# Attention's product with V: from two rounded fp32 parts per head to plain fp32 in four column tiles

## The chip, the cores and the metric

The kernel runs on one core of one Trainium2 chip. Its time is the device time of one execution in microseconds (us). Engines are named as in the profile: PE is TensorE's matmul, PEld its weight load, DVE is VectorE, ACT is ScalarE, POOL is GpSimd, SP is SyncE, whose queue issues nearly all DMAs.

## What is computed

A block of attention with a memory over four segments, and behind it a channel MLP, all in float32. The change touches only `a_dot`, the product of the softmax with V:

```python
# x: (1, 2048, 1024); H = 32 heads of Dh = 32; N = 4 segments of L = 512
h = x + _A_ref(_layernorm(x), wq, wk, wv, wo, beta)
out = h + _B_ref(_layernorm(h), w1, b1, w2, b2)

# _A_ref, for each segment s
logits = jnp.einsum("bhqd,bhkd->bhqk", qs, ks) * scale + mask     # causal
p = _softmax(logits, axis=-1)
a_dot = jnp.einsum("bhqk,bhkd->bhqd", p, vs)
pq = phi(qs)
a_mem = (pq @ M) / (pq @ z + 1e-6)
o = g * a_mem + (1.0 - g) * a_dot                                 # g = sigmoid(beta), per head
M = M + phi(ks).T @ vs;  z = z + phi(ks).sum()
# at the end: concat(o) @ wo
```

## The kernel before

**Units.** The sequence is done in two halves of two segments each. Attention of a half runs over 8 groups of four heads, and in a group over its two segments: 16 units a half, 32 in all. A unit is one group in one segment. Its dense part (`dense`, L432) projects K, Q and V, 24 steps of three 512-column matmuls each (L124 to L126, one for each pair of a rounded high part and a rest). While it runs, the heads of the unit before are done beside it: `interleave` (L816) takes one step of `heads` after each dense step. Further work of a unit hangs on these steps by the table `TIMES` (L33): at step `ck`, for instance, the key weights of the next group are cast, at `lk` they are loaded.

**A head.** Each head takes a slot of six steps, and the table `HEAD` (L34) says at which step each of its operations stands; a number of 6 or more means a later slot, in which the next head has already begun. `qk` (L652) makes the logits for four blocks of 128 queries (128 to 512 keys each), adds the mask on DVE and takes the exponential on ACT. `ptr` (L696) transposes the weights `pr` in three groups into PSUM banks `ppt`, 10 transposes a head. ACT rounds each group into `pth` (float32r), and `sub` (L714) has DVE put the rest into `ptl`. `av` (L718) multiplies: for each of four blocks of keys, `vs` stands as weights, 64 columns that hold V's rounded part (32) and its rest (32), and `pth` and `ptl` stream through, 8 matmuls a head into the bank `po`. ACT copies the lower half of `po` into `ot` (L734), and `av_out` (L736) adds the upper half on DVE. At the fourth head POOL multiplies `ot` by `w` (L743). `weigh` (L681) makes `w`, which holds gate over sum for each query: a transpose `pw`, a copy, a DMA out to `r_dram` (L691) and four DMAs back (L693).

**Small matmuls.** Reading and updating the memory M takes 24 small matmuls in a unit that has both (`pm`, `pmm`, L425). They are kept in a list, and `one_small` takes one of them in front of a transpose (10 places a head) or of a product (7 places).

**What sets the order.** Engines take their instructions in the order of the program, which a scheduler may change where dependencies leave it room; `in_order` (L104) fixes the written order. The attention units ran without it.

Of the kernel before, what the change touches and what calls it, by code (L numbers as in the profile page):

```python
# [17 lines left out]
P = 128  # L18
# [11 lines left out]
RA, RH, RS, PD, PS = 1.3, 14, 0.7, 20, 3  # L30
VT, KT, OT = True, True, True
WLC = 8
TIMES = dict(pk=10, kx=12, pkh=21, pkl=22, ks=11, qs=16, pq=16, pqh=20, pql=20, omt=20, vx=24, pm=25, vs=32, vl=33, pmm=40, om=35, omc=40, od=62, lk=13, lq=16, lv=20, ck=18, cq=22, cv=28)  # L33
# [14 lines left out]
def build(tc, x, wq, wk, wv, wo, beta, w1, b1, w2, b2, out):  # L48
# [52 lines left out]
        getattr(nc, lo_eng).tensor_tensor(lo, w, raw(hi), op=ALU.subtract)  # L101

    @contextmanager
    def in_order(*engines):  # L104
# [12 lines left out]
        acts["last"] = last  # L117

    def behind(op):

# [232 lines left out]
    def attention(half, first):  # L353
# [293 lines left out]
                yield  # L647

        offs = [0, 128, 384, 768]
        koff = [0, 512, 1024, 896]  # L650

        def qk(st, i):  # L652
            u, j = st["u"], st["j"]
# [41 lines left out]

        def ptr(st, n):  # L696
            grp = ((0,), (1, 3), (2,))[n]
            if n == 0:
                st["pth"] = ab.tile([P, 1280], F32R, name="pth", bufs=2)
                st["ptl"] = ab.tile([P, 1280], F32R, name="ptl", bufs=2)  # L700
            pr, pth, ptl = st["pr"], st["pth"], st["ptl"]
            ppt = psum.tile([P, 512], F32, tag="pt", name="ppt", bufs=2)
            base = koff[grp[0]]
            w = 0
            for jk in grp:
                for i in range(jk, 4):
                    one_small()
                    o = koff[jk] - base + (i - jk) * P
                    nc.tensor.transpose(ppt[:, o:o + P], pr[:, offs[i] + jk * P:offs[i] + (jk + 1) * P], ident)  # L709
                    w += P  # L710
            acts["pth"] = n, nc.scalar.copy(pth[:, base:base + w], ppt[:, :w])  # L711
            st["sub", n] = (ptl[:, base:base + w], ppt[:, :w], raw(pth[:, base:base + w]))

        def sub(st, n):  # L714
            o, x0, x1 = st["sub", n]
            nc.vector.tensor_tensor(o, x0, x1, op=ALU.subtract)  # L716

        def av(st, n):  # L718
            u, j = st["u"], st["j"]
            if n == 0:  # L720
                st["po"] = psum.tile([P, 512], F32, tag="av", name="po", bufs=1)[0:64, :]
            po = st["po"]
            for jk in (0, 1) if n == 0 else (3, 2):
                w = 512 - P * jk
                v = u["vs"][:, 4 * j + jk, :]
                for part in ("pth", "ptl"):
                    if (jk, part) != (3, "ptl"):
                        one_small()
                    nc.tensor.matmul(po[:, P * jk:], v, st[part][:, koff[jk]:koff[jk] + w],  # L729
                                     start=(jk, part) == (0, "pth"), stop=(jk, part) == (2, "ptl"))  # L730
            if n == 1:
                if j == 0:
                    u["ot"] = ab.tile([P, 512], F32, name="ot", bufs=1)
                nc.scalar.copy(u["ot"][32 * j:32 * j + 32, :], po[32:64, :])  # L734

        def av_out(st):  # L736
            u, j, po = st["u"], st["j"], st["po"]
            ot = u["ot"]
            b = slice(32 * j, 32 * j + 32)
            nc.vector.tensor_tensor(ot[b, :], po[0:32, :], ot[b, :], op=ALU.add)  # L740
# [18 lines left out]

        stages = int(max(HEAD.values())) // 6  # L760
        pipe = [None] * stages
        fns = {"q": qk, "r": inverse, "w": weigh, "t": ptr, "s": sub, "a": av, "o": av_out}

        def slot(cur):
            states = [cur] + pipe
# [836 lines left out]
```

## Time and profile before

| What | Value |
|---|---|
| Median of the three runs shown | 2276.23 us |
| Lowest and highest run | 2275.69 and 2284.74 us |
| Profiled execution: span, first to last instruction | 2272.7 us |
| Attention of the first half, first and last product with V | 58.7 and about 539 us |
| Attention of the second half, first and last product with V | about 919 and 1396.7 us |
| DVE rows of L716 (`ptl`) | 384 of 595 ns mean |
| ACT rows of L711 (`pth`) | 384 of 512 ns mean |

The page gives the span of the profiled execution; what lies around it is seen only as the distance to the median, 3.5 us. A line of the page's groups reads: source line, engine, operation, output and inputs by the program's names, forms, count; then busy time and mean duration of one in ns; then how long the engine sat idle ahead of them, and what ended that. In a timeline the columns are start and duration in us, engine, line, operation and form; like neighbours stand in one row with their count.

### The profile page before, as it was taken

What the parts mean: (1) busy time and instruction counts of PE and PEld (TensorE: products, weight loads), DVE (VectorE), ACT (ScalarE), POOL (GpSimd) and SP (SyncE); (2) the same over time, 40 slices, a digit from 0 to 9 for tenths busy, and PEclk for the clock granted to TensorE, in tenths of its full rate; (3) what the DMA queues carried; (4) which work ended last, traced back from release to release, by engine and by line L of the source; (5) the groups of instructions that cost most, each with busy time, mean ns of one, the idle gap of its engine ahead of it and who ended that gap; (6) DMA issues with size and microseconds to landing.
All of it is one profiled execution on the core that took longest, in us unless ns stands there. A gap on an engine that the chain in (4) does not pass through costs nothing.

```text
span 2272.7 us, 34849 instructions
## 1 busy us (share of the span) xinstructions
PE 2243.7 (99%) x11481; PEld 1861.9 (82%) x11481; DVE 1541.0 (68%) x3073; ACT 1232.8 (54%) x2553; POOL 856.8 (38%) x710
## 2 busy tenths in 40 slices
PE   8999999999999999999999999999999999999999
PEld 6888888877888888888888887888888888888887
DVE  6777777776656565777777787655666766567653
ACT  6777777774453445777777775453334223222221
POOL 4232233334244442233333334244445654055430
PEclk9999999999999999999999999999999999999999
DMA  6666666665475655666655565466568975476762
GB/s 215 182 190 181 181 179 176 177 177 196 139 212 165 189 167 173 195 177 179 178 173 169 178 195 189 142 210 181 162 177 310 331 253 197 155 257 226 244 234 89
DMA packets 400798, 437.41 MB, mean 192 GB/s; under 512 B 33102, under 2 KB 267114, under 8 KB 400618
## 3 DMA queue, kind: packets, MB, share of 16 engines
q1 hardware_dynamic: 337450, 398.48, 56.8%
q10 hardware_dynamic: 63168, 36.71, 5.4%
q8 instruction: 91, 1.49, 0.3%
q14 instruction: 89, 0.73, 0.1%
HBM read 287.41 MB, written 128.78 MB: 183 GB/s over the span
## 4 chain that ended last, share of the span: by engine, by line
PE 86%; DMA 4%; POOL 3%; ACT 2%; DVE 2%; issue 1%; SPq 1%; POOLq 0%; ACTq 0%; DVEq 0%
PE po L1436 22%; PE bps L1040 10%; PE cps L1040 7%; PE dps L1040 7%; PE po L729 6%; PE ppt L709 5%; PE pqk L659 3%; PE qps L124 3%; PE qps L125 2%; PE kps L124 2%; PE qps L126 2%; PE vps L124 2%; PE kps L126 2%; PE kps L125 2%; PE vps L125 2%; PE vps L126 2%
## 5 line engine op out<-in xcount | busy, mean ns | idle before, releaser
L668 ACT ACTIVATE pr<-pr,mx 128x128 f32<-128x128 f32 (+3 forms) x512 | 289.1, 565 | 107.3 <-DVE mx L660 104.0
L660 DVE CUSTOM_DVE_ANT_0 pr<-pqk,mask 128x128 f32<-128x128 f32 (+3 forms) x512 | 247.2, 484 | 87.0 <-PE pqk L659 82.2
L711 ACT CAST pth<-ppt 128x512 fp32r<-128x512 f32 (+1 forms) x384 | 194.9, 512 | 91.3 <-PE ppt L709 88.9
L716 DVE TENSOR_TENSOR ptl<-ppt,pth 128x512 fp32r<-128x512 f32 (+1 forms) x384 | 226.8, 595 | 14.5 <-ACT pth L711 11.9
L709 PE MATMUL ppt<-ident,pr 128*128 128x128 f32 x1280 | 217.4, 276 | 0.7 <-DVE ptl L716 0.4
L1446 DVE TENSOR_TENSOR c<-c,po 128x512 f32<-128x512 f32 x160 | 105.4, 683 | 149.0 <-PE po L1436 147.2
L709 PEld LDWEIGHTS ppt<-ident,pr 128*128 128x128 f32 x1280 | 163.9, 140 | 36.7 <-issue 2.2
L659 PE MATMUL pqk<-ks,qs 96*128 96x128 f32 (+3 forms) x512 | 183.0, 358 | 1.1 <-DVE mx L660 1.1
L799 POOL TENSOR_TENSOR wl<-wr,wh 128x1024 fp32r<-128x1024 f32 x42 | 101.1, 2406 | 179.1 <-ACT wh L797 132.0
L729 PE MATMUL po<-ptl,vs 128*64 128x512 f32 (+3 forms) x512 | 153.1, 308 | 1.9 <-DVE ptl L716 1.9
L729 PE MATMUL po<-pth,vs 128*64 128x512 f32 (+3 forms) x512 | 147.8, 309 | 2.9 <-DVE ot L740 1.6
L1436 PE MATMUL po<-w2h,zh 128*128 128x512 f32 x378 | 121.0, 390 | 0.2 <-DVE zh L1376 0.2
L1040 PE MATMUL bps<-zh,sb 128*128 128x512 f32 x336 | 111.1, 391 | 0.0
L1293 POOL TENSOR_TENSOR w2r<-w2r 128x512 f32<-128x512 f32 x54 | 85.4, 1590 | 68.3 <-DMA w2r<-in_B_w 45.4
L1040 PE MATMUL bps<-zh,sa 128*128 128x512 f32 x336 | 110.9, 391 | 0.0
L124 PE MATMUL kps<-yh,wh 128*128 128x512 f32 (+1 forms) x264 | 109.9, 416 | 0.0
L124 PE MATMUL qps<-yh,wh 128*128 128x512 f32 x256 | 107.8, 421 | 0.0
L124 PE MATMUL vps<-yh,wh 128*128 128x512 f32 x256 | 106.2, 415 | 0.0
L659 PEld LDWEIGHTS pqk<-ks,qs 96*128 96x128 f32 x512 | 98.2, 192 | 8.3 <-DVE mx L660 1.8
L1436 PE MATMUL po<-w2h,hl 128*128 128x512 f32 x322 | 103.3, 390 | 0.4 <-DVE hl L1376 0.4
L125 PE MATMUL kps<-yl,wh 128*128 128x512 f32 (+1 forms) x264 | 102.8, 389 | 0.1
L126 PE MATMUL kps<-yh,wl 128*128 128x512 f32 (+1 forms) x264 | 102.9, 390 | 0.0
(251 smaller groups left out, 6527.8 us busy)
## 6 DMA issues: line engine op xcount, KB each, us to landing
hr<-h_dram SPq DMA_DIRECT2D x112, 448.0 KB, 5.3
w2r<-in_B_w SPq DMA_DIRECT2D x122, 256.0 KB, 4.3
r<-in_B_w SPq DMA_DIRECT2D x56, 512.0 KB, 4.5
ks<-ks_dram SPq DMA_DIRECT2D x128, 192.0 KB, 3.1
h_dram<-ht ACTq DMA_DIRECT2D x84, 256.0 KB, 3.7
ks_dram<-kh SPq DMA_DIRECT2D x64, 256.0 KB, 2.6
wr<-in_A_wo SPq DMA_DIRECT2D x32, 512.0 KB, 4.5
wx<-in_B_w SPq DMA_DIRECT2D x56, 256.0 KB, 3.5
```

The costliest lines, as they stand in the source:

```text
L124: nc.tensor.matmul(ps, ah, bh, start=first, stop=False)
L125: nc.tensor.matmul(ps, ah, bl, start=False, stop=False)
L126: acts["mm"] = nc.tensor.matmul(ps, al, bh, start=False, stop=last)
L659: nc.tensor.matmul(pqk[:, :n], u["qs"][j][:, i * P:(i + 1) * P], u["ks"][j][:, 0:n], start=True, stop=True)
L660: nc.vector.tensor_tensor_reduce(out=st["pr"][:, offs[i]:offs[i] + n], in0=pqk[:, :n], in1=mask[:, 512 - n:512], op0=ALU.add, op1=ALU.min, ...
L668: nc.scalar.activation(pi, pi, AF.Exp, bias=mx[:, i:i + 1], scale=-1.0, accum_out=mx[:, 4 + i:5 + i])
L709: nc.tensor.transpose(ppt[:, o:o + P], pr[:, offs[i] + jk * P:offs[i] + (jk + 1) * P], ident)
L711: acts["pth"] = n, nc.scalar.copy(pth[:, base:base + w], ppt[:, :w])
L716: nc.vector.tensor_tensor(o, x0, x1, op=ALU.subtract)
L729: nc.tensor.matmul(po[:, P * jk:], v, st[part][:, koff[jk]:koff[jk] + w], start=(jk, part) == (0, "pth"), stop=(jk, part) == (2, "ptl"))
L1040: nc.tensor.matmul(ps, x_[:, c, :], y_[:, c, :], start=first and c == 0 and n == 0, stop=last and c == 3 and n == 2, skip_group_check=True)
L1436: nc.tensor.matmul(ps, x_[:, k], y_[k], start=opens and k == 0 and i == 0, stop=closes and k == self.KP - 1 and i == 2, skip_group_check=True)
```

## The change

`sub` goes, and with it the rounding: `ptr` copies each group of transposes as plain float32 into `pt`, the first group on DVE, the two others on ACT (L710, L712 of the changed kernel). `pt` has four buffers for each group, so that it lasts for the four heads of a unit. `av` does nothing for the first three heads. At the fourth it takes one block of keys, `jk`, at a time: four plain fp32 matmuls, one for each head, with V itself (`vn`, 32 columns) as weights, each in its own 32 columns of the array (`tile_position=(0, 32 * j)`) and into its own 32 partitions of one bank `po`. That is 16 calls a unit, 512 in all, in place of 1024. DVE multiplies `po` by `w` (L732), where ACT, DVE and POOL made and used `ot`. The order of PE inside units is fixed as written, and the `TIMES` of the weight loads and casts are 3 to 10 steps smaller. `vs` is still made, for the update of M.

Compiled, the old program has 11481 matmul instructions on PE, as the page counts them, and the changed one has 11481 too: 1024 calls went and 512 came, so each plain fp32 call is two instructions, each with its own weight load. The two of a call stand next to each other, ahead of those of the next tile.

```diff
-TIMES = dict(..., om=35, omc=40, od=62, lk=13, lq=16, lv=20, ck=18, cq=22, cv=28)
-HEAD = dict(r=6.1, q0=1.1, a0=14.1, s2=14.2, t0=8.3, q2=2.4, s0=8.5, a1=15.1, q1=3.2, t1=10.1, w=9.2, q3=4.3, t2=11.1, o=17.2, s1=11.3)
+TIMES = dict(..., om=35, omc=40, od=62, lk=3, lq=8, lv=13, ck=11, cq=18, cv=25)
+HEAD = dict(r=6.1, q0=1.1, a0=13.1, a1=14.1, a2=15.2, a3=15.1, t0=8.3, q2=2.4, q1=3.2, t1=10.1, w=11.2, q3=4.3, t2=11.1, o=17.2)
...
         def ptr(st, n):
             grp = ((0,), (1, 3), (2,))[n]
...
+            u, j, pr = st["u"], st["j"], st["pr"]
+            w = sum(P * (4 - jk) for jk in grp)
+            pt = ab.tile([P, w], F32, name=f"pt{n}", bufs=4)
             ppt = psum.tile([P, 512], F32, tag="pt", name="ppt", bufs=2)
...
-            acts["pth"] = n, nc.scalar.copy(pth[:, base:base + w], ppt[:, :w])
-            st["sub", n] = (ptl[:, base:base + w], ppt[:, :w], raw(pth[:, base:base + w]))
-
-        def sub(st, n):
-            o, x0, x1 = st["sub", n]
-            nc.vector.tensor_tensor(o, x0, x1, op=ALU.subtract)
...
-                for part in ("pth", "ptl"):
-                    if (jk, part) != (3, "ptl"):
-                        one_small()
-                    nc.tensor.matmul(po[:, P * jk:], v, st[part][:, koff[jk]:koff[jk] + w],
-                                     start=(jk, part) == (0, "pth"), stop=(jk, part) == (2, "ptl"))
-            if n == 1:
-                if j == 0:
-                    u["ot"] = ab.tile([P, 512], F32, name="ot", bufs=1)
-                nc.scalar.copy(u["ot"][32 * j:32 * j + 32, :], po[32:64, :])
+                nc.vector.tensor_copy(pt, ppt[:, :w])
+            else:
+                nc.scalar.copy(pt, ppt[:, :w])
+
+        def av(st, jk):
+            u = st["u"]
+            if st["j"] < 3:
+                return
+            if jk == 0:
+                u["po"] = psum.tile([P, 512], F32, tag="av", name="po", bufs=1)
+            v = u["v"]["vn"].rearrange("p (h k e) -> p h k e", h=4, k=4)
+            ops = []
+            for j in range(4):
+                ops.append(nc.tensor.matmul(u["po"][32 * j:32 * j + 32, P * jk:], v[:, j, jk, :], u["pt", jk][j],
+                                            start=jk == 0, stop=jk == 2, tile_position=(0, 32 * j)))
+            for a, b in zip(ops, ops[1:]):
+                tc.add_manual_dep(b.ins, a.ins.name, NOSYNC, reason="program order")
...
-            nc.vector.tensor_tensor(ot[b, :], po[0:32, :], ot[b, :], op=ALU.add)
-            if j == 3:
+            if st["j"] == 3:
                 w = u["w"]
-                nc.gpsimd.tensor_tensor(w, ot, w, op=ALU.mult)
+                nc.vector.tensor_tensor(w, u["po"], w, op=ALU.mult)
...
-                    interleave(d, heads(prev), 1.0)
+                    with in_order(mybir.EngineType.PE, keep=False):
+                        interleave(d, heads(prev), 1.0)
```

The first place is PE in the fourth unit, where its queries (`qps`) begin. Before, a head's first four products stand here, two for each of the two key blocks:

```order
L126 MATMUL kps<-yh_204,wl 128x512
L659 MATMUL pqk<-ks,qs 128x128
L124 MATMUL qps<-yh_204,wh 128x512
L125 MATMUL qps<-yl_205,wh 128x512
L126 MATMUL qps<-yh_204,wl 128x512
L729 MATMUL po<-pth,vs 64x512
L729 MATMUL po<-ptl,vs 64x512
L729 MATMUL po<-pth,vs 64x384
L729 MATMUL po<-ptl,vs 64x384
L709 MATMUL ppt<-ident,pr 128x128 x4
L659 MATMUL pqk<-ks,qs 128x384
```

The same place on PE of the changed kernel (its lines are one higher up to here; `pt_1391` and the like are the buffers of the four heads, `sch` holds V):

```order
L723 MATMUL po<-pt_1391,sch 32x512
L723 MATMUL po<-pt_1485,sch 32x512
L723 MATMUL po<-pt_1599,sch 32x512
L723 MATMUL po<-pt_1673,sch 32x512
L659 MATMUL pqk<-ks,qs 128x128
L125 MATMUL qps<-yh_204,wh 128x512
L126 MATMUL qps<-yl_205,wh 128x512
L127 MATMUL qps<-yh_204,wl 128x512
L723 MATMUL po<-pt_1424,sch 32x384
L723 MATMUL po<-pt_1534,sch 32x384
L723 MATMUL po<-pt_1624,sch 32x384
L723 MATMUL po<-pt_1699,sch 32x384
```

All products of a unit now stand in one slot: four calls of width 512, four of 384, and after three more dense matmuls four of 128 and four of 256 without anything between them. The dense matmuls and `pqk` keep their order.

The second place is PE in the same unit, where the update of the memory (`pmm`) is worked off during the values. Before, the small matmuls stand between products:

```order
L425 MATMUL pmm<-vs,pkh 128x128
L729 MATMUL po<-pth,vs 64x512
L425 MATMUL pmm<-vs,pkh 128x128
L729 MATMUL po<-ptl,vs 64x512
L425 MATMUL pmm<-vs,pkl 128x128
L729 MATMUL po<-pth,vs 64x384
L425 MATMUL pmm<-vs,pkh 128x128
L729 MATMUL po<-ptl,vs 64x384
```

On PE of the changed kernel the rows at that place are:

```order
L426 MATMUL pmm<-vs,pkh 128x128
L707 MATMUL ppt<-ident,pr 128x128
L426 MATMUL pmm<-vs,pkh 128x128
L707 MATMUL ppt<-ident,pr 128x128
L426 MATMUL pmm<-vs,pkl 128x128
L707 MATMUL ppt<-ident,pr 128x128
L426 MATMUL pmm<-vs,pkh 128x128
L707 MATMUL ppt<-ident,pr 128x128
```

The small matmuls keep their order and stand in front of transposes only.

The third place is DVE over about one head of a unit in steady state. Before, it holds the eviction of logits (L660), the subtractions and the add of `ot`:

```order
L660 ISA pr,mx<-pqk,mask 128x384
L660 ISA mx 128x1
L716 TENSOR_TENSOR ptl<-ppt,pth 128x512
L660 ISA pr,mx<-pqk,mask 128x256
L660 ISA mx 128x1
L740 TENSOR_TENSOR ot<-po,ot 32x512
L660 ISA pr,mx<-pqk,mask 128x512
L660 ISA mx 128x1
L716 TENSOR_TENSOR ptl<-ppt,pth 128x512
```

On DVE of the changed kernel, a head with the multiplication by `w`, which stands there once a unit:

```order
L710 COPY pt_1873<-ppt 128x512
L660 ISA pr,mx<-pqk,mask 128x384
L660 ISA mx 128x1
L732 TENSOR_TENSOR scl<-po,scl 128x512
L660 ISA pr,mx<-pqk,mask 128x256
L660 ISA mx 128x1
L493 TENSOR_TENSOR ql<-qps,qh 128x512
```

One copy of `ppt` a head takes the place of three subtractions, and the multiplication stands between two evictions.

On SP the load of the value weights now stands ahead of the stacking of keys (`ks`) of the same unit, and behind it before; the transfers of `w` (L691, L693) keep their place between the transfers of turned values.

More of the change, by code (lines that the diff above doesn't have):

```diff
@@ L32 @@
 WLC = 8
-TIMES = dict(pk=10, kx=12, pkh=21, pkl=22, ks=11, qs=16, pq=16, pqh=20, pql=20, omt=20, vx=24, pm=25, vs=32, vl=33, pmm=40, om=35, omc=40, od=62, lk=13, lq=16, lv=20, ck=18, cq=22, cv=28)
-HEAD = dict(r=6.1, q0=1.1, a0=14.1, s2=14.2, t0=8.3, q2=2.4, s0=8.5, a1=15.1, q1=3.2, t1=10.1, w=9.2, q3=4.3, t2=11.1, o=17.2, s1=11.3)
+TIMES = dict(pk=10, kx=12, pkh=21, pkl=22, ks=11, qs=16, pq=16, pqh=20, pql=20, omt=20, vx=24, pm=25, vs=32, vl=33, pmm=40, om=35, omc=40, od=62, lk=3, lq=8, lv=13, ck=11, cq=18, cv=25)
+HEAD = dict(r=6.1, q0=1.1, a0=13.1, a1=14.1, a2=15.2, a3=15.1, t0=8.3, q2=2.4, q1=3.2, t1=10.1, w=11.2, q3=4.3, t2=11.1, o=17.2)
 KD, QD = 0, 3
@@ L103, in in_order @@
     @contextmanager
-    def in_order(*engines):
+    def in_order(*engines, keep=True):
         traced = nc.cur_bb.bb.instructions
@@ L116, in in_order @@
             last[ins.engine] = ins
-        acts["last"] = last
+        if keep:
+            acts["last"] = last
     def behind(op):
@@ L697, in ptr @@
             grp = ((0,), (1, 3), (2,))[n]
[L698 to L701, printed above, removed]
+            u, j, pr = st["u"], st["j"], st["pr"]
+            w = sum(P * (4 - jk) for jk in grp)
+            pt = ab.tile([P, w], F32, name=f"pt{n}", bufs=4)
             ppt = psum.tile([P, 512], F32, tag="pt", name="ppt", bufs=2)
-            base = koff[grp[0]]
@@ L714, in sub @@
-        def sub(st, n):
-            o, x0, x1 = st["sub", n]
-            nc.vector.tensor_tensor(o, x0, x1, op=ALU.subtract)
-        def av(st, n):
-            u, j = st["u"], st["j"]
-            if n == 0:
[L721 to L725, printed above, removed]
-                for part in ("pth", "ptl"):
-                    if (jk, part) != (3, "ptl"):
-                        one_small()
-                    nc.tensor.matmul(po[:, P * jk:], v, st[part][:, koff[jk]:koff[jk] + w],
-                                     start=(jk, part) == (0, "pth"), stop=(jk, part) == (2, "ptl"))
-            if n == 1:
-                if j == 0:
-                    u["ot"] = ab.tile([P, 512], F32, name="ot", bufs=1)
-                nc.scalar.copy(u["ot"][32 * j:32 * j + 32, :], po[32:64, :])
@@ L761, in attention @@
         pipe = [None] * stages
[L762 removed]
+        fns = {"q": qk, "r": inverse, "w": weigh, "t": ptr, "a": av, "o": av_out}
         def slot(cur):
```

11 lines of the change are left out of this document (4 added, 7 removed).

## The prediction

> **What bounds the kernel now.** I read the page's first part, then the chain, then PE's waits, then PE's timeline inside attention.
>
> ```profile
> span 2272.7 us, 34849 instructions
> PE 2243.7 (99%) x11481; PEld 1861.9 (82%) x11481; DVE 1541.0 (68%) x3073; ACT 1232.8 (54%) x2553; POOL 856.8 (38%) x710
> ...
> PE 86%; DMA 4%; POOL 3%; ACT 2%; DVE 2%; issue 1%; SPq 1%; POOLq 0%; ACTq 0%; DVEq 0%
> PE po L1436 22%; PE bps L1040 10%; PE cps L1040 7%; PE dps L1040 7%; PE po L729 6%; PE ppt L709 5%; PE pqk L659 3%; PE qps L124 3%; PE qps L125 2%; PE kps L124 2%; PE qps L126 2%; PE vps L124 2%; PE kps L126 2%; PE kps L125 2%; PE vps L125 2%; PE vps L126 2%
> ```
>
> TensorE is the chain, and the product with V (L729) is 6% of it. A busy PE could still hide waiting, so the windows view of the first half's attention comes next (columns: length, then busy time and instructions of PE, PEld, DVE, ACT, POOL), and then PE's waits (total us, times, longest).
>
> ```profile
> 47.00:563.00 516.00, 508.91 (x2973) 424.58 (x2972) 386.78 (x1052) 377.44 (x930) 167.00 (x169) 0.99 0.63 182
> ```
>
> ```profile
> PE pt L277 <- ACT xt L267: 9.7, 2, 8.5
> ...
> PE po L729 <- DVE ptl L716: 1.9, 2, 1.1
> PE po L729 <- DVE ot L740: 1.6, 3, 0.9
> PE po L729 <- DVE vs L539: 1.2, 2, 0.8
> ```
>
> PE is busy 508.9 of 516 us there, at a granted clock of 0.99, while DVE and ACT have over a quarter of the time free. The waits at L729 are 1.9 + 1.6 + 1.2 = **4.7 us** in the whole run. So what counts is how long PE's own stream is: each ns of PE work taken out or put in moves the end by about as much, and DVE or ACT work taken out moves nothing.
>
> **The change part by part. (a) The old product goes.** A matmul's listed time overlaps the next one's; its price is the distance from its start to the next start. PE's timeline (start, length, engine, line, what, form):
>
> ```profile
> 392.66 0.22 PE L729 MATMUL po<-pth,vs 128*64 128x128 f32 x1
> 392.72 0.22 PE L729 MATMUL po<-ptl,vs 128*64 128x128 f32 x1
> 392.78 0.28 PE L729 MATMUL po<-pth,vs 128*64 128x256 f32 x1
> 392.90 0.28 PE L729 MATMUL po<-ptl,vs 128*64 128x256 f32 x1
> 393.01 0.29 PE L659 MATMUL pqk<-ks,qs 96*128 96x256 f32 x1
> ...
> 397.41 0.40 PE L126 MATMUL kps<-yh,wl 128*128 128x512 f32 x1
> 397.64 0.40 PE L729 MATMUL po<-pth,vs 128*64 128x512 f32 x1
> 397.88 0.39 PE L729 MATMUL po<-ptl,vs 128*64 128x512 f32 x1
> 398.11 0.33 PE L729 MATMUL po<-pth,vs 128*64 128x384 f32 x1
> 398.28 0.34 PE L729 MATMUL po<-ptl,vs 128*64 128x384 f32 x1
> 398.45 0.60 PE L709 MATMUL ppt<-ident,pr 128*128 128x128 f32 x4
> 398.80 0.42 PE L659 MATMUL pqk<-ks,qs 96*128 96x384 f32 x1
> 399.06 0.40 PE L124 MATMUL kps<-yh,wh 128*128 128x512 f32 x1
> ```
>
> A head costs 0.24 + 0.23 + 0.17 + 0.17 (widths 512 and 384) and 0.06 + 0.06 + 0.12 + 0.11 (128 and 256): 1.16 us. 32 units of 4 heads: 128 x 1.16 = **148.5 us** leave PE, and the 4.7 us of waits with them.
>
> **(b) What a plain fp32 matmul costs.** The old program has no such matmul. The nearest row is the transpose of pr, plain fp32 too.
>
> ```profile
> L709 PE MATMUL ppt<-ident,pr 128*128 128x128 f32 x1280 | 217.4, 276 | 0.7 <-DVE ptl L716 0.4 <-ACT pr L668 0.3
> ...
> L729 PE MATMUL po<-ptl,vs 128*64 128x128 f32 x128 | 28.5, 222 | 0.0
> ```
>
> Over the same 128 columns it takes 54 ns longer than the rounded operand of L729 (276 to 222). In the timeline, four of them and the 384-wide pqk take 398.45 to 399.06, 0.61 us; with 0.17 for 384 columns, 0.44 is left, **0.11 us for 128 columns**, against 0.06 rounded. Each of the 512 new calls is two matmul instructions (the instruction counts in the section on the change). At 0.11 per 128 columns one of the two takes 0.44, 0.33, 0.22 or 0.11 us at widths 512, 384, 256 and 128; twice the rounded price of (a) gives about 0.46, 0.34, 0.23, 0.12, which is the upper end.
>
> **(c) How far the four tiles overlap** decides the sign. In every row above, PE starts matmuls strictly in program order. The program puts the two halves of one tile's call side by side, then the next tile's. Both halves need the same columns of the array, so the second waits for the first; in an in-order stream the next tile's first half stands behind it and starts with it. Then only the second half of one tile runs beside the first half of the next: four tiles need five lengths, not two and not eight. Per unit: 5 x 0.44 for width 512, 5 x 0.33 for 384, and, since 128 and 256 follow without a gap, 4 x 0.11 + 5 x 0.22: 5.39 us. 32 units: **172.5 us**, from 169 (the merged row of four transposes gives (0.60 - 0.276) / 3 = 0.108 us) to 180 (twice the rounded price).
>
> The Trainium skill, "TensorE: Matmul & The Clock Gate", section "Part 3: Packing small matmuls — row/col tiling", says that matmuls keep program order in start and in end, and gives 2.38 times for three column tiles 512 wide. The trace agrees on the order of starts, and shows no column tiles; the page's own case has one instruction per tile, so by its order rule two halves in a row give my five lengths, by its speed-up alone a sum nearer to the first rival.
>
> **(d) Going into and out of the tiles.** Three bursts a unit, six changes, 192 in all. If each drained the array, it would cost what the next start hides at 397.41: 0.40 long but 0.23 apart, so 0.17 us, 32 us in all. The nearest row, from transposes back to rounded matmuls, loses nothing beyond (b); I take 0 and keep 32 as upper end; below zero nothing can lie, since there is no such change now. The Trainium skill, "TensorEngine Tiling (Array Packing)", section "Key Properties", says that a change of tiling mode drains TensorE; by it the sum would lie toward that upper end, and no row here shows one.
>
> **(e) The small matmuls** (pm, pmm) that stood between old products now stand between transposes.
>
> ```profile
> 386.13 0.29 PE L709 MATMUL ppt<-ident,pr 128*128 128x128 f32 x1
> 386.18 0.31 PE L425 MATMUL pmm<-vs,pkl 128*128 128x128 f32 x1
> 386.32 0.30 PE L709 MATMUL ppt<-ident,pr 128*128 128x128 f32 x1
> ...
> 390.16 0.22 PE L425 MATMUL pmm<-vs,pkh 128*128 128x128 f32 x1
> 390.22 0.39 PE L729 MATMUL po<-pth,vs 128*64 128x512 f32 x1
> ```
>
> Among products one costs 0.06; a transpose with one costs 0.19 (386.13 to 386.32), so 0.08 of its own. At most 7 of 17 places a head were among products, 7/17 of 576: 237 x 0.02 = **5 us**; 0 is the lower end.
>
> **(f) What is costed at nothing.** The 384 subtractions (L716), the rounding copies and the small adds of ot leave DVE and ACT, which have room; of them only the 4.7 us were ever waited for. PE's order by hand: the order of the old program is already the written one at the places shown, so 0, with up to 5 us either way. The weight loads and casts come 3 to 10 steps earlier; PE's waits name no wl at all in attention, so there is nothing to win. The cast of k (1.05 us on ACT) and its subtraction (2.4 us on POOL) must free a buffer before the load of v, which is queued two steps behind the cast as before; behind it on SP wait the key stacks of the unit in work, which are used half a unit later. DVE now multiplies po by w: this one can wait (last rival).
>
> ```profile
> L797 ACT CAST wh<-wr x28: 1030/1050/1056, 45.3 to 1291.1; 128x1024 fp32r<-128x1024 f32 x28
> ...
> L799 POOL TENSOR_TENSOR wl<-wr,wh x42: 2387/2398/2737, 46.4 to 1292.2; 128x1024 fp32r<-128x1024 f32 x42
> ```
>
> **Sum:** -148.5 - 4.7 + 172.5 + 0 + 5 = +24.3 us on the span of 2272.7, which is 2297.0; the median of the runs shown (2276.2) lies 3.5 above that span, so **2300 us**. This case's own range is 2286 (169 us, nothing for small matmuls, 5 us won by the order) to 2340 (180 us and the drains).
>
> **The rivals.** **Four tiles at once (not slower).** If a tile's second half can queue at its own columns while other tiles start, four tiles need two lengths: 2 x (0.44 + 0.33 + 0.11 + 0.22) = 2.2 us a unit, 70.4 in all; -148.5 - 4.7 + 70.4 + 5 = -77.8, **2198 us**; from 2192 (0.108, nothing for small matmuls) to 2230 (with the drains). For it: nothing in PE's rows excludes a second queue, as none addresses part of the columns. Against it: no start ever passes an earlier one. The point that decides is 148 us of product: below 4.6 us a unit the change wins. The Trainium skill's "Key Properties" of the tiling page, by which tiles run matmuls in parallel and independently, is what speaks for this time; no run here shows it yet.
>
> **The tiles take turns (the change does not do what it says).** Eight lengths: 8.8 us a unit, 281.6 us: -153.2 + 281.6 + 5 = +133, **2410 us**. For it: plain fp32 streams could fill the path that feeds the array. Against it: one such stream needs a new column only half as often as the rounded one (0.11 to 0.06).
>
> **DVE stuck at w (slower still).** w returns from DRAM by two transfers queued on SP after pw. Their landing times (min/median/max), the write and then the reads:
>
> ```profile
> DMA to landing us min/median/max: 1.3/2.8/4.9
> ```
>
> ```profile
> DMA to landing us min/median/max: 1.9/2.3/5.8
> ```
>
> Usually 5 us, at worst 11. pw stands six steps ahead of the multiplication, a quarter of a unit of some 30 us (516 us hold the half's 16), 7.5 us, plus the 5.4 us of products between: 12.9 us. Only if SP's queue adds more than 2 us to the worst landing does DVE stop, and the evictions of pqk behind it; 2 us in each of 32 units on top of my forecast would be 2364 us.
>
> **How the numbers follow.** Five lengths 0.47, two lengths 0.36, turns 0.14, DVE 0.03. The forecast is 2300 us. To leave out no more than 0.2, the range takes in the first rival and leaves out the last two: 2192 to 2340. A measurement of this kernel tells about 0.5% (11 us) from no change; of the five lengths the lowest part, 2286 to 2287.6, and cases where drains and order offset each other fall within it, 0.08. Faster 0.36, same 0.08, slower 0.56.
>
> **What would show it.** On the new page PE keeps 11481 matmuls and stays near 99%. In its timeline at a burst, starts of the two halves 0.44 us apart at width 512, with the next tile's first half beginning beside the second half, mean my case; all first halves within a tenth of a us the first rival; eight starts 0.44 apart that never share the array, the second. A gap before the first po or the matmul behind the burst prices (d). PE's waits for DVE mx grow if DVE is stuck. I am wrong above all if the four tiles of a burst end within 1 us at width 512.

## The result, and the profile after

| | Median of four runs | Lowest and highest |
|---|---|---|
| before | 2276.56 us | 2275.69 and 2284.74 |
| changed | 2258.74 us | 2256.48 and 2265.45 |

The ratio is 0.9924, with a 95% interval of 0.9897 to 0.9951: the change makes the kernel 0.76% faster, 17.8 us. The forecast was 2300 us, on the other side of no change; the time lies inside the range only because the range takes in the first rival, the four tiles at once.

The page of the changed kernel begins as follows (busy time, share of the span and instructions of each engine). The execution profiled is the slowest of the four; the spans of the other three are 2254.4 to 2258.2 us, so sums over this trace show 5 to 9 us less gain than the usual run has. Its mean granted clock is 0.992 where the other three have 0.994 and 0.995; 0.0025 of 2263 us are about 6 us, so most of that difference is clock (an estimate).

```profile
span 2263.5 us, 34026 instructions
PE 2218.5 (98%) x11481; PEld 1779.1 (79%) x11481; DVE 1382.1 (61%) x2721; ACT 1082.0 (48%) x2297; POOL 807.6 (36%) x678
...
L707 PE MATMUL ppt<-ident,pr 128*128 128x128 f32 x1280 | 236.0, 283 | 3.7 <-ACT pr L668 2.4
...
L710 DVE COPY pt<-ppt 128x512 f32<-128x512 f32 x128 | 88.3, 690 | 78.9 <-PE ppt L707 78.9
L712 ACT COPY pt<-ppt 128x512 f32<-128x512 f32 (+1 forms) x256 | 119.8, 468 | 23.8 <-PE ppt L707 21.7
```

PE keeps its 11481 matmuls and falls from 99% to 98%. DVE lost 159 us of work and ACT 151, and neither shows in the time: as forecast, PE's stream decides. The copies of `ppt` wait for PE (78.9 us on DVE); the transposes wait 3.7 us in all, and last 283 ns on the average where they lasted 276.

**The burst.** PE's timeline at the products of one unit (start, length, engine, line, what, form, count):

```profile
362.63 0.40 PE L126 MATMUL kps<-yl,wh 128*128 128x512 f32 x1
362.86 0.40 PE L127 MATMUL kps<-yh,wl 128*128 128x512 f32 x1
363.19 1.07 PE L723 MATMUL po<-pt,sch 128*32 128x512 f32 x8
364.18 0.33 PE L659 MATMUL pqk<-ks,qs 96*128 96x128 f32 x1
364.35 0.45 PE L125 MATMUL qps<-yh,wh 128*128 128x512 f32 x1
364.64 0.40 PE L126 MATMUL qps<-yl,wh 128*128 128x512 f32 x1
364.88 0.40 PE L127 MATMUL qps<-yh,wl 128*128 128x512 f32 x1
365.20 0.85 PE L723 MATMUL po<-pt,sch 128*32 128x384 f32 x8
365.99 0.33 PE L426 MATMUL pm<-mzl,pqh 128*128 128x132 f32 x1
```

Eight matmuls of 512 columns end 1.07 us after the first starts. Five lengths of 0.44 would be 2.2 us, eight 3.5; this is two. The eight starts within that row, as the trace has them, in ns from the first (with the modelled duration):

```
0 (617)    7 (617)   14 (617)   20 (617)
454 (592)  460 (592)  467 (592)  474 (592)
```

Four matmuls start within 20 ns and four more 454 ns later, when the columns come free. Two halves of one call cannot start 7 ns apart in the same columns (the tile-major run below has 453 ns between them), so the first row is the four first halves. In the program a call's halves stand side by side, `A A B B C C D D`; on the array they run `A B C D A B C D`. PE lets the next tile pass a waiting second half; the tile-major run shows the same by the widths of its matmuls alone. That is the rival "four tiles at once".

The same rows price the way in and out of the tiles. From the last dense matmul to the first product 0.33 us (362.86 to 363.19), where dense matmuls are 0.23 apart: 0.10. From the last product, 474 ns behind 363.19, to `pqk` at 364.18 0.52 us, where the 0.43 would do that lie between two halves of this width in the runs below: 0.09. From that 128-wide `pqk` to the next dense matmul 0.17, where the old trace has 0.06 (a 128-wide product to the next): 0.11. Together **about 0.3 us a burst**, and there are 96 bursts: 28 us. `e3_full_array` below, which uses no tiles, checks it at the same place: 0.23 us ahead of the products and 0.49 from the last one to the dense matmul behind `pqk`, where the changed kernel has 0.33 and 0.69, so 0.30 more.

**Where the gain stayed.** The distance from each start on PE to the next, summed by what the matmul writes, after minus before:

| Writes | us | Writes | us |
|---|---|---|---|
| `po`, product with V | -69.8 (157.5 to 87.7) | `kps`, `qps`, `vps` | +14.2 |
| `pwo`, product with wo | +15.9 | `ppt` | +3.8 |
| `pm`, `pmm` | +12.5 | everything else | about +3 |
| `pqk` | +11.2 | **span** | **-9.2** |

Of what the products gave, 60 us went back into their neighbours. Part is the way in and out, which falls on the matmul beside a burst. Part is the stage behind the units: from the last dense matmul of a half to the next stage, PE does the heads of the last unit and the product with wo. The windows view of these stretches, before and then after (columns: length, then busy time and instructions of PE, PEld, DVE, ACT, POOL, then granted clock, DMA share, GB/s):

```profile
484.30:606.00 121.70, 113.93 (x560) 92.77 (x559) 78.08 (x139) 57.04 (x103) 40.55 (x42) 0.97 0.50 163
1348.20:1463.30 115.10, 109.94 (x549) 89.22 (x548) 78.60 (x137) 56.25 (x101) 39.33 (x40) 1.00 0.51 166
```

```profile
468.30:606.40 138.10, 126.91 (x577) 96.56 (x576) 73.06 (x123) 52.84 (x93) 39.24 (x43) 0.90 0.48 160
1329.00:1452.20 123.20, 112.95 (x564) 87.59 (x563) 72.13 (x124) 52.18 (x96) 41.18 (x40) 0.99 0.48 161
```

In the first half the units end 16.0 us earlier (484.3 to 468.3), and the next stage begins 0.3 us later: the whole gain of that half is gone in this run. In the second half the units are 19.5 us shorter (467.9 to 448.4 from the first dense matmul to the last) and the stretch behind them 8.1 longer. In the first half PE idles 11.2 us of 138.1 where it idled 7.8 of 121.7. It is also busy 13.0 us longer on nearly the same work, and the clock says why: 0.90 of 138.1 us leaves out 13.8 us of full clock, 0.97 of 121.7 leaves out 3.7. By this estimate **about 10 of the 16 us are clock**, 3.4 are waits, and the rest is work. Part of that clock belongs to this one execution: `e7_old_loads` and `e2_one_burst` below leave this stretch as it is and have 132.9 and 133.0 us there, at 0.96. In the second half the clock stays at 0.99, and of the 8.1 us 5.1 are waits (10.3 us idle, 5.2 before). The same view in short stretches just behind the last dense matmul of the first half, the last three set to where the clock changes:

```profile
470.20:473.60 3.40, 3.40 (x34) 1.62 (x34) 0.69 (x1) 1.14 (x3) 1.27 (x1) 1.00 0.51 124
473.60:477.00 3.40, 2.55 (x15) 1.26 (x10) 1.74 (x7) 1.63 (x6) 0.00 (x0) 1.00 0.99 366
478.18:481.59 3.41, 3.41 (x15) 2.89 (x16) 2.30 (x10) 3.25 (x12) 0.00 (x0) 0.50 0.99 344
481.59:485.01 3.42, 1.97 (x12) 1.14 (x10) 3.06 (x9) 3.08 (x10) 1.12 (x1) 1.00 0.11 40
485.01:495.25 10.24, 9.28 (x30) 6.41 (x31) 5.09 (x12) 6.03 (x14) 2.18 (x2) 0.50 0.09 23
```

PE pauses for 0.85 us of the stretch from 473.60 to 477.00, and from 478.18 the clock is half for 3.41 us; it is full again for as long, PE idles 1.45 us of that, and then it is half for 10.24 us. But pauses alone do not say when it falls. In the second half, two stretches with more of them, 1.47 and 2.23 us, are each followed by one at full clock:

```profile
1346.00:1349.40 3.40, 1.93 (x10) 1.53 (x9) 2.68 (x6) 2.96 (x10) 1.74 (x1) 1.00 0.13 23
1349.40:1352.80 3.40, 3.40 (x17) 2.82 (x16) 0.00 (x0) 0.00 (x0) 0.00 (x0) 1.00 0.97 243
1363.00:1366.40 3.40, 1.17 (x6) 0.49 (x3) 1.08 (x1) 3.03 (x4) 1.99 (x1) 1.00 0.00 0
1366.40:1369.80 3.40, 2.97 (x13) 2.47 (x14) 2.50 (x3) 0.00 (x0) 2.62 (x2) 1.00 0.49 148
```

In the old kernel wo's first matmul stood 0.4 us behind the last dense one (484.64 behind 484.27) and filled the pauses of the heads. Now, in the first half, it starts at 492.1, 24 us behind. PE's waits for the whole run (total us, times, longest) name what it stood on:

```profile
PE pwo L126 <- POOL wl L101: 9.2, 5, 1.9
PE pwo L126 <- POOL zl L101: 3.0, 2, 1.5
...
PE pwo L125 <- ACT zh L100: 2.4, 2, 1.2
PE ppt L707 <- ACT pr L668: 2.4, 6, 0.7
```

The waits of `pwo` for its weights add up to 15.6 us, and to 7.5 in the old kernel. They lie in these two stretches: 7.0 of the 11.2 us that PE idles in the first half, 8.7 of 10.3 in the second (2.9 in the old kernel). No row names a wait for `mx` or `w` above 0.2 us: the DVE rival did not come about.

### The profile page after: what moved, and what is told of

Same layout as the page of the kernel before. It is cut to its first block, busy times and chain, and to the rows that moved or that the text cites. A ratio compares the mean times of both kernels' runs of the same rounds, so it can differ in the third digit from the quotient of the medians.

```text
span 2263.5 us, 34026 instructions
## 1 busy us (share of the span) xinstructions
PE 2218.5 (98%) x11481; PEld 1779.1 (79%) x11481; DVE 1382.1 (61%) x2721; ACT 1082.0 (48%) x2297; POOL 807.6 (36%) x678
## 4 chain that ended last, share of the span: by engine, by line
PE 87%; DMA 4%; POOL 2%; DVE 2%; issue 2%; ACT 1%; SPq 1%; ACTq 0%; POOLq 0%; DVEq 0%
PE po L1426 21%; PE bps L1030 9%; PE cps L1030 7%; PE ppt L707 6%; PE dps L1030 6%; PE pqk L659 4%; PE po L723 4%; PE qps L125 3%; PE vps L125 3%; PE vps L126 2%; PE kps L125 2%; PE vps L127 2%; PE qps L127 2%; PE qps L126 2%; PE kps L127 2%; PE kps L126 2%
## 5 line engine op out<-in xcount | busy, mean ns | idle before, releaser
L660 DVE CUSTOM_DVE_ANT_0 pr<-pqk,mask 128x128 f32<-128x128 f32 (+3 forms) x512 | 241.1, 483 | 101.0 <-PE pqk L659 99.6
L707 PE MATMUL ppt<-ident,pr 128*128 128x128 f32 x1280 | 236.0, 283 | 3.7 <-ACT pr L668 2.4
L659 PE MATMUL pqk<-ks,qs 96*128 96x128 f32 (+3 forms) x512 | 188.8, 371 | 1.6 <-DMA qs<-ql 1.3
L710 DVE COPY pt<-ppt 128x512 f32<-128x512 f32 x128 | 88.3, 690 | 78.9 <-PE ppt L707 78.9
L712 ACT COPY pt<-ppt 128x512 f32<-128x512 f32 (+1 forms) x256 | 119.8, 468 | 23.8 <-PE ppt L707 21.7
L126 PE MATMUL vps<-yl,wh 128*128 128x512 f32 x256 | 101.6, 397 | 0.0
L127 PE MATMUL vps<-yh,wl 128*128 128x512 f32 x256 | 101.2, 395 | 0.0
```

Source lines behind the costliest of these rows:

```text
L126: nc.tensor.matmul(ps, ah, bl, start=False, stop=False)
L127: acts["mm"] = nc.tensor.matmul(ps, al, bh, start=False, stop=last)
L659: nc.tensor.matmul(pqk[:, :n], u["qs"][j][:, i * P:(i + 1) * P], u["ks"][j][:, 0:n], start=True, stop=True)
L660: nc.vector.tensor_tensor_reduce(out=st["pr"][:, offs[i]:offs[i] + n], in0=pqk[:, :n], in1=mask[:, 512 - n:512], op0=ALU.add, op1=ALU.min, ...
L712: nc.scalar.copy(pt, ppt[:, :w])
```

## The experiments

Each run is timed in three rounds beside the old kernel on the same chip; ratios are to that.

**How the tiles overlap.** `e3_full_array` gives each call all 128 columns, so that calls follow one another; it leaves out that the heads stay apart.

```diff
-ops.append(nc.tensor.matmul(u["po"][32 * j:32 * j + 32, P * jk:], v[:, j, jk, :], u["pt", jk][j],
-                            start=jk == 0, stop=jk == 2, tile_position=(0, 32 * j)))
+ops.append(nc.tensor.matmul(u["po"][:, P * jk:], u["v"]["vn"][:, P * j:P * j + P], u["pt", jk][j],
+                            start=(jk, j) == (0, 0), stop=(jk, j) == (2, 3)))
```

> The same 16 calls of a unit in the same widths, plain fp32, but each over all 128 columns of the array, with 128 columns of V as weights, all four heads added up in the whole bank; it leaves out that the heads stay apart. No tiles, so nothing can run at once. My theory: eight lengths in place of two, 8 x (0.433 + 0.325 + 0.217 + 0.108) = 8.7 us a unit in place of 2.2 and without the 0.29 us at each burst: 32 x 6.5 - 28 = +180 us, about 2438. Rival (a half of a plain fp32 call costs no more than a rounded matmul, and the tiles gain little): 4.6 us a unit in place of 2.7, about 2300.

Measured: 2421.77 us (2420.52 to 2423.23), ratio 1.0652 (1.0630 to 1.0674). Its halves start 0.43, 0.32, 0.11 and 0.22 us apart at widths 512, 384, 128 and 256: eight lengths, as in the prediction's rival of tiles that take turns (2410 us; 2438 was expected here). With plain fp32 and no tiles the kernel is 6.5% slower than the old one; the tiles are worth 163 us to the changed kernel.

`e8_tile_major` keeps the tiles and changes only the order: all four calls of a head stand together, then the next head's.

```diff
-HEAD = dict(..., a0=13.1, a1=14.1, a2=15.2, a3=15.1, ...)
+HEAD = dict(..., a0=14.1, ...)
...
             for j in range(4):
-                ops.append(nc.tensor.matmul(u["po"][32 * j:32 * j + 32, P * jk:], v[:, j, jk, :], u["pt", jk][j],
-                                            start=jk == 0, stop=jk == 2, tile_position=(0, 32 * j)))
+                for jk in (0, 1, 3, 2):
+                    ops.append(nc.tensor.matmul(u["po"][32 * j:32 * j + 32, P * jk:], v[:, j, jk, :], u["pt", jk][j],
+                                                start=jk == 0, stop=jk == 2, tile_position=(0, 32 * j)))
```

> One burst a unit, with the calls of one tile (eight instructions) all ahead of the next tile's, in place of four tiles after each other. Theory of a free look-ahead (each tile has its own stream, and PE takes the next instruction of any free tile from what is queued): as the single burst, 2241, all four tiles starting together. Theory of a short look-ahead (it reaches past one instruction of a busy tile, not past seven): the first tile runs seven of its eight alone, four tiles take between five and eight lengths, 3 to 6 us more a unit: 2340 to 2440. My forecast of these: the short one.

Measured: 2382.99 us (2380.43 to 2384.64), ratio 1.0468 (1.0449 to 1.0487). PE's timeline of one burst:

```profile
303.54 0.39 PE L127 MATMUL qps<-yh,wl 128*128 128x512 f32 x1
303.86 6.94 PE L723 MATMUL po<-pt,sch 128*32 128x512 f32 x32
310.73 0.66 PE L707 MATMUL ppt<-ident,pr 128*128 128x128 f32 x4
```

The 32 matmuls take 6.87 us. Their starts in ns, from the trace, with the first tile's above:

```
tile A: 0  453  883  1205  1528        1637  1746  1962
tile B:                          1533                    1987  2416 ...
```

Tile B's first matmul, 512 wide, starts ahead of A's last three, which are 128 and 256 wide, and as soon as only those three of A's still wait; C and D follow B and C in the same way. In this run PE looks past three waiting matmuls and never past four. In the order of the change, `A A B B C C D D`, D's first half has to pass exactly three waiting ones. Here the three wait for one tile, there for three tiles; no run has four waiting for different tiles, so whether the limit counts them all together or those of one tile is not shown. Of the two theories the short look-ahead came about, inside its 2340 to 2440 us. So both the forecast's rule and "tiles run on their own" are wrong in general, and the order inside the burst is worth 140 us between this run and the next.

**The way in and out.** `e2_one_burst` puts the three bursts of a unit into one, in the order of the change.

```diff
-HEAD = dict(..., a0=13.1, a1=14.1, a2=15.2, a3=15.1, ...)
+HEAD = dict(..., a0=14.1, a1=14.12, a3=14.14, a2=14.16, ...)
```

> The changed kernel with all 16 calls of a unit at one place of the order in place of three. My theory: each time PE goes into the tiles and out of them costs 0.29 us (0.10 ahead of the first po, 0.09 behind the last, 0.10 at the next matmul), so two bursts fewer in 32 units are worth 64 x 0.29 = 18.6 us: 2240 us. Rival (the gaps are waits for operands or for a free bank, and not the change of tiles): the gaps move along with the calls, within 5 us of 2258.7; if the longer burst starves the exponentials, above it.

Measured: 2241.30 us (2239.86 to 2249.86), ratio **0.9865** (0.9840 to 0.9890), the shortest median of all runs (the ratio of `e6_all` below, 0.9860, is no different). PE's timeline of one burst:

```profile
300.66 0.40 PE L127 MATMUL qps<-yh,wl 128*128 128x512 f32 x1
300.99 2.36 PE L723 MATMUL po<-pt,sch 128*32 128x512 f32 x32
303.28 0.33 PE L426 MATMUL pm<-mzl,pqh 128*128 128x132 f32 x1
```

All products of a unit take 2.29 us (300.99 to 303.28), by two lengths and one exit. 64 bursts went, and 17.4 us between the medians (2258.74 to 2241.30), 0.27 us a burst; by the ratios to the old kernel timed beside each it is 13 us, 0.21. The other two pairs that differ in this alone were each timed together: 16.7 us from `e5_tail_order` to `e6_all`, 17.1 from `e9_four_early` to `e10_four_burst` (below), 0.26 and 0.27 us a burst. The rival, gaps that move along with the calls, did not come about.

**The order of PE.** `e1_no_pe_order` is the changed kernel without the fixed order in units; `e11_before_ordered` is the old kernel with it.

```diff
-                    with in_order(mybir.EngineType.PE, keep=False):
-                        interleave(d, heads(prev), 1.0)
+                    interleave(d, heads(prev), 1.0)
```

> The changed kernel without the fixed order of PE inside the attention units. My theory (the four tiles do run at once, and the gain is eaten by entering and leaving the tiles and by a later wo stage, neither of which the fixed order causes): within 8 us of the changed kernel's 2258.7, that is 2251 to 2267, and the stretch from the last dense matmul of the first half to the stage behind wo stays near 138 us. Rival (the fixed order of PE is what holds the wo stage back): that stretch goes back to 122 us, and the time to about 2242.

Measured: 2363.50 us (2356.37 to 2366.66), ratio 1.0390 (1.0365 to 1.0415). Both expectations fell, and the stretch behind the first half's units takes 151 us, neither 138 nor 122: left to the scheduler, the new product would have lost. The windows view of the same stretch of attention, with the order (first fence) and without:

```profile
47.00:465.00 418.00, 414.11 (x2577) 322.38 (x2577) 259.79 (x778) 265.77 (x719) 110.38 (x122) 0.99 0.65 183
```

```profile
47.00:465.00 418.00, 402.51 (x2339) 301.28 (x2338) 224.82 (x694) 230.47 (x640) 101.83 (x115) 0.96 0.57 159
```

Without it PE idles 15.5 us there, where it idled 3.9, has 0.96 of the clock and gets through 2339 matmuls in place of 2577. PE's waits for the whole run now name rows that were at most 2.4 us each in the changed kernel:

```profile
PE pqk L659 <- DMA qs<-ql: 9.1, 3, 4.2
...
PE ppt L707 <- DVE pt L710: 6.5, 11, 1.6
PE ppt L707 <- ACT pr L668: 6.2, 15, 0.9
PE pm L426 <- POOL pql L514: 5.3, 7, 0.9
```

The transposes alone take 36.5 us more from start to start, the dense part of the two halves 36 and 39 us more. In one piece of the timeline, 303.8 to 309 us, logits and transposes stand together and PE idles 1.10 us for DVE's `mx` and 0.75 for the copy `pt`; that this is how the scheduler's order loses the time is read from there and not tested by itself.

```diff
...
-                    interleave(d, heads(prev), 1.0)
+                    with in_order(mybir.EngineType.PE, keep=False):
+                        interleave(d, heads(prev), 1.0)
```

> The kernel before, with nothing changed but PE's order fixed as written inside the attention units. My theory (the old program already ran in nearly that order; the fixed order only undoes what the new product does to the scheduler's choice): within 8 us of the kernel before, 2266 to 2283. Rival (the fixed order is a gain by itself, and the product is not): 2262 or less.

Measured: 2282.37 us (2277.24 to 2285.32, ten runs), ratio 1.0032 (1.0019 to 1.0046). On the old kernel the order gains nothing and costs 0.3%. So the order alone is not the gain, and the new product without it is a loss; the 0.76% takes both.

**The weight loads.** `e7_old_loads` is the changed kernel with the old `TIMES` of loads and casts.

```diff
-TIMES = dict(..., lk=3, lq=8, lv=13, ck=11, cq=18, cv=25)
+TIMES = dict(..., lk=13, lq=16, lv=20, ck=18, cq=22, cv=28)
```

> The changed kernel with the weight loads and casts at their steps of before. My theory (PE never waits for these weights, in either kernel): within 6 us of the changed kernel, 2253 to 2265. Rival (the earlier casts are what keeps the shorter units fed): 2270 or more, with waits of PE for wl or wh.

Measured: 2266.95 us (2260.80 to 2271.07), ratio 0.9959 (0.9945 to 0.9973), against 0.9924 (0.9897 to 0.9951) with the new ones. It lies between the two expectations, and PE's waits name no weight of the units. The intervals overlap by a little: the earlier loads are worth 8 us or nothing. This stays open, and with it how much of the 17.8 us is the product's; no run has the old product with the earlier loads.

**The stage behind the units.** Three runs tried to win back the 16 and 8 us. `e4_wo_early` loads and splits the first two blocks of wo during the last unit.

```diff
+                        d = hooked(d, wo_early, 1, 24)
...
+    def wo_early(n):
+        if n == 0:
+            acts["early"] = [wo_raw(0, k) for k in (0, 1)]
+        if n in (9, 17):
+            k = (n - 9) // 8
+            acts["home", k] = wo_halves(acts["early"][k], k, wo_home())
...
```

> The changed kernel with the first two blocks of the weights of wo loaded and split during the last attention unit of a half, as their buffers come free, and not behind it. My theory (after the last dense matmul PE finds no wo weights and runs the rest of the heads alone, one behind the other): PE goes on with wo at once, the stretch from the last dense matmul to the stage behind wo falls from 138 to about 125 us in the first half, 12 to 16 us less in all: 2243 to 2247. Rival (the stretch is long because the heads' own chain from exponential to product is): less than 4 us, 2255 or more.

Measured: 2264.79 us (2261.67 to 2271.61), ratio 0.9962 (0.9946 to 0.9977). No gain: the rival's "2255 or more". In the first half wo's first matmul now stands 0.4 us behind the last dense one, and the stretch takes 133.4 us, no less than the 132.9 and 133.0 of the runs that leave it alone.

`e5_tail_order` adds to it a fixed order of PE in that stage, with `vn` and `w` of the last group in buffers of their own, and `e6_all` adds the one burst.

```diff
-        interleave(wo_first(half, hts, pre()), rest, RA, RH, RS)
+        with in_order(mybir.EngineType.PE, keep=False):
+            interleave(wo_first(half, hts, pre()), rest, RA, RH, RS)
```

> The changed kernel with the order of PE fixed as written behind the units too, where the last heads run beside the product with wo; for that V and w of the last group stand in buffers of their own, and the first two wo blocks are loaded early. My theory (the change upsets the order that the scheduler finds; inside the units the fixed order mends it, behind them nothing does, and 16 and 8 us are lost there): the stretch from the last dense matmul to the stage behind wo falls from 138 and 123 to 120 and 112 us, 25 to 30 us less: 2230 to 2236 beside 2258.7. Rival (the stretch is long because wo's weights are split late on POOL, whatever the order): it stays above 130 and 120, and the time above 2250.

> The tail in order as in the run beside it, and one burst a unit. My theory: the two gains add up, 2258.7 - 17 - 27 = about 2215. Rival (one of them is only the other's loss moved): no better than 2230.

Measured: 2261.37 us (2260.22 to 2269.39), ratio 0.9942 (0.9923 to 0.9961), and 2244.65 us (2241.68 to 2246.93), ratio 0.9860 (0.9837 to 0.9882). Neither beats the kernel without these edits. The stretches of `e5_tail_order` are 134.5 and 118.6 us, where 120 and 112 were expected. PE's longest wait in `e5_tail_order` is a new one, for the third block of wo:

```profile
PE pwo L125 <- ACT wh L100: 10.2, 1, 10.2
PE pqk L659 <- DVE mx L660: 6.7, 4, 3.4
PE pwo L126 <- POOL wl L101: 3.8, 2, 1.9
```

`e9_four_early` therefore loads the next two blocks early too (`wo_early` gets the line `acts["early"].append(wo_raw(0, k + 2))`, and `wo_first` takes the last two blocks from there), and `e10_four_burst` is that with one burst.

> As the run with the ordered tail, but the last two wo blocks too are loaded during the last attention unit, each as the block two before it has been split and leaves its buffer. There PE stood 10 us for the third block, whose load waited on SP behind the query stacks. My theory (order and weights both have to be in time, and each alone gives little): the stretch from the last dense matmul to the stage behind wo falls to 118 us in the first half and 113 in the second, the time to 2238 to 2246. Rival (that stretch is bound by the last heads' chain or by the work on ACT and POOL): 2255 or more.

> The same with one burst a unit. My theory: 18 us less than the run beside it, 2220 to 2228. Rival: as the single burst alone, 2241.

Measured: 2265.04 us (2259.75 to 2265.91), ratio 0.9950 (0.9934 to 0.9965), and 2247.91 us (2244.04 to 2250.63), ratio 0.9881 (0.9858 to 0.9905). Again the rivals: 2255 or more, and no better than the single burst alone. In `e9_four_early` the 10.2 us are gone, and others stand in their place. PE's waits in the first half's stretch, and the windows view of it, which still has 0.90 of the clock and more idling than in the changed kernel (15.4 us of 133.5):

```profile
PE pw L688 <- DVE om L552: 4.5, 1, 4.5
PE pwo L125 <- ACT zh L100: 3.3, 1, 3.3
PE pwo L126 <- POOL wl L101: 1.9, 1, 1.9
```

```profile
467.90:601.40 133.50, 118.06 (x577) 90.94 (x576) 69.36 (x125) 53.64 (x98) 41.03 (x40) 0.90 0.51 168
```

Set side by side, the lengths of the units (first dense matmul to last) and of the stretch behind them, in us, tell where the runs that load wo early lost again what they won:

| Run | Units, first half | Stretch behind | Units, second half | Stretch behind |
|---|---|---|---|---|
| before | 468.9 | 121.7 | 467.9 | 115.1 |
| changed | 452.5 | 138.1 | 448.4 | 123.2 |
| `e7_old_loads` | 457.0 | 132.9 | 448.3 | 123.0 |
| `e2_one_burst` | 443.2 | 133.0 | 439.9 | 122.6 |
| `e4_wo_early` | 453.9 | 133.4 | 454.4 | 124.3 |
| `e5_tail_order` | 455.1 | 134.5 | 454.5 | 118.6 |
| `e6_all` (one burst) | 446.0 | 128.9 | 446.9 | 119.3 |
| `e9_four_early` | 454.2 | 133.5 | 456.0 | 119.7 |
| `e10_four_burst` (one burst) | 446.9 | 131.4 | 448.6 | 119.3 |

Each is to be read against the run with as many bursts, `changed` or `e2_one_burst`. In the second half the early loads with the ordered tail win 3.3 to 4.6 us; in `e5_tail_order` and `e9_four_early` PE's waits for wo there fall from 8.7 us to 3.7 and 3.9, so these waits are part of the 8 us. But in all five runs with early loads the units ahead are 6.0 to 8.7 us longer, and PE waits in them 3.6 to 5.1 us for `mx`, where `changed` has no such wait and `e2_one_burst` 0.5 us; why `mx` comes late is not shown. In the first half the stretch stays between 128.9 and 138.1 us in all of them. What is left as a suspicion are the chains of the last four heads (logits, exponential, transposes, all ahead of the products that need all four) and the clock. No run took these away, so the cause of the 16 and 8 us is not settled.

## Why the prediction was wrong, step by step

**(c), the overlap of the tiles, is the step that failed.** It reasoned that "in an in-order stream the next tile's first half stands behind it and starts with it", hence five lengths, 172.5 us. The rows behind it were right: every start shown did follow the program. But none of them had a matmul waiting for columns while another had free ones, so they could not show whether PE would let one pass. It does, up to three: the four tiles take two lengths in place of five, and all products 87.7 us with their exits in place of 172.5. The five lengths were the likeliest case only because the absence of such a row was read as evidence. The rule of the Trainium skill ("TensorE: Matmul & The Clock Gate", section "Part 3: Packing small matmuls — row/col tiling") that matmuls start and end in program order, which was put beside it, does not hold in these traces: starts of 0, 7, 14 and 20 ns above can't be made in program order, nor can the 512-wide start ahead of three narrower ones in `e8_tile_major`. It would give five lengths here; the measurement decides.

**(a) and (b) held.** The old products took 157.5 us from start to start, against 148.5 and 4.7 of waits. The first two halves of a burst lie 454 and 347 ns apart at widths 512 and 384; inside the longer burst of `e2_one_burst` it is 429 and 322, against 0.44 and 0.33.

**(d), taken as 0, is 28 us** (0.3 us for each of 96 bursts; 0.27 by `e2_one_burst`). Its upper end, 32, was near it. The row it leaned on, transposes back to rounded matmuls, changes the operand's type but not the tiles. That the Trainium skill's page "TensorEngine Tiling (Array Packing)", section "Key Properties", has a change of tiling mode drain the engine agrees with these rows: 0.3 us for two changes, where the upper end had taken 0.17 for each.

**(e), 5 us, is 12.5 us** by the summed distances of `pm` and `pmm`; the part that stands right behind a burst pays the way out, which belongs to (d).

**(f), nothing, has two halves.** DVE's and ACT's work, 159 and 151 us less, shows in no row of PE's as a gain, though no run isolates it. The order of PE is nothing on the old kernel (+0.3%) but 105 us on the changed one, which was not foreseen: the price of an order was taken from the old kernel, where a scheduler happened to give nearly the same.

**The first rival** had the mechanism, and 2198 us (2230 with the drains) for 2258.74. What it lacked are the drains it took as an upper end (28 us), the rest of (e) (7.5), and the stage behind the units: 16 and 8 us in the profiled run, which no step of the prediction looked at. These come to 2258; the profiled run itself took 2265.45, so some 7 us of it have no name here. The tiles did not take turns, and DVE was not stuck. The lower end of the five lengths comes out at 2287 by the prediction's own terms, not 2286; nothing hangs on it.

## What to carry to other kernels

In these runs column tiles in plain fp32 overlap fully where the next tile's first instruction is no more than three waiting matmuls away, so write them one instruction or one call per tile in turn, and put all bursts that can stand together into one, since each cost 0.3 us to enter and leave. Where a new product changes what the scheduler does, try it with the order fixed as well: here that decided the sign. When PE is the bound and its work gets shorter, look at the end of the stage too: what used to hide under it (here the last heads and the loads of the next weights) surfaces there, and pauses can cost clock on top. Compare the stages one by one: loads moved out of that stage won up to 4.6 us there and lost 6 to 9 in the stage ahead. And where a trace has no row in which two instructions could have passed each other, it says nothing on their order; such a case deserves even chances.

## What was not expected of the hardware

- PE starts a matmul for free columns past up to three matmuls that wait for theirs, out of program order: starts 0, 7, 14, 20 ns, and 1533 ns in the tile-major order (6.87 us in place of 2.29).
- Going into and out of column tiles cost 0.3 us here: 0.10 ahead of the first product, 0.09 behind the last, 0.11 behind the matmul that follows.
- The clock fell without any long pause: 0.85 us of short ones in a stretch of 3.4 us (three, the longest 0.49), then half clock for 3.41 us, and soon after for 10.24. It did not fall behind 1.47 and 2.23 us of pauses elsewhere in the same trace. What decides between them no run isolates.
